# Gated mix of two attentions: three row tiles projected in the main loop instead of ahead of it, and the lead's maxima taken in pairs

## The chip, the cores and the metric

One core of one Trainium2 chip runs the program. The metric is the device time of one execution in microseconds (us): 2651.11 us is the median of three runs of the kernel before (2650.65 to 2652.03). A difference of some 0.2% (5.3 us) is about the least that a measurement of this kernel tells from none.

## The reference

Two attentions over the same 2048 rows x (576 wide), each with 32 heads of 18 elements, are mixed by a gate. A has a key and a value of its own for each head; B shares one key and one value among its 32 heads.

```python
def _A_ref(x, wqkv, wo):          # 32 heads, own k and v each
    scores = jnp.einsum("bhqd,bhkd->bhqk", q, k) * scale
    p = _softmax(scores, axis=-1)
    o = jnp.einsum("bhqk,bhkd->bhqd", p, v)
    return o.transpose(0, 2, 1, 3).reshape(B, S, D) @ wo
def _B_ref(x, wq, wk, wv, wo):    # the same with one k and one v: "bhqd,bkd->bhqk"
...
g = _sigmoid((x * gate_w).sum(-1, keepdims=True))
return g * _A_ref(A_x, ...) + (1 - g) * _B_ref(A_x, ...)
```

## The kernel before

**Number format.** Nearly everything is float32 made of two parts (high and low), so a projection is 14 matrix products: 12 of 128 rows for the first 512 elements of x (high by high, low by high, high by low) and two for the remaining 64, whose high and low parts share one 128-row tile.

**Rows.** All the row vectors that the scores need (B's key, the gate's logit, B's value, B's 32 queries, then query and key of each head of A) stand as 14 tiles of 128 rows in `wall`. Projecting a tile makes 128 x 2048 numbers, in 512-column groups, and sends their high and low parts to `qk_d` in DRAM. From there the main loop loads each head's 18 query rows three times (high, high, low, 54 partitions), and the keys in the same way, on partitions 0 to 53 (`SB`) and again on 64 to 117 (`MB`).

**Stages.** (1) Tiles 0, 1 and 2 are projected while x arrives and is split (`split_x`), 512 columns at a time: order tile 0, 1, 2 within each of four column groups c. PSUM has seven banks to turn through, and the projections use three of them in turn. (2) Tile 3, four groups, during which the rows of tile 0 come back from DRAM (`bring_row`, 26 loads). (3) The **lead**: tiles 4 to 7, sixteen groups; after each group come six matmuls for the row maxima of the first 22 row tiles (`step_max`, L645), which VectorE reduces (L654); ScalarE copies the group out (L300) and GpSimd splits it. `store_x` writes the split x to DRAM for later, eight stores. (4) The **main loop**, 64 heads of 16 steps. Per step: four score matmuls (L690, letter s) on the array's lower 64 rows, beside four for the maxima 22 steps ahead (m) on its upper 64 rows; four exponentials on ScalarE (L698); four reductions on VectorE; and four quarters of the sums with the values (L705, the digits) over all 128 rows. In every second row, one difference product replaces two maxima: x is a product with the difference of two key halves, whose Relu ScalarE writes (L648), and y joins it with the other half in one VectorE instruction (L651): max(a, b) = b + Relu(a - b).

**Units.** What is not attention runs within the main loop as units: 32 of the values of A (14 products), seven for each remaining row tile (14 products of 292 columns), and the output projection (12 products of 288). A unit is executed in 64-row halves (`half_step`, L906): the letters A (rows 64 to 127) and B (rows 0 to 63), each a product of 64 rows, so that they stand beside the scores and maxima. A's sum is copied by ScalarE, B's is added by VectorE (L881).

**Order.** The order on TensorE is written out as strings of eight steps each. PLAIN has no unit, HALF14 one of 14 products, HALF12 one of 12, DENSE four of 12; `emit` chooses by the step T. Per eight steps every string has 32 s, 24 m, 4 x, 4 y and 32 quarters, and the quarters divide it in groups: ten in PLAIN and HALF12, nine in HALF14, seven in DENSE. Six tiles (8 to 13) are units in `row_units`, T from 282 to 618; the values stand from T=18 to 274, the first half of the output projection from 634 to 890, the second in DENSE from 946. A planner (`Clock`) chooses each matmul's PSUM bank as the program is written; it moves nothing on the chip.

Of the kernel before, what the change touches and what calls it, by code (L numbers as in the profile page):

```python
# [8 lines left out]
F32 = mybir.dt.float32  # L9
# [18 lines left out]
LEAD = 22  # L28
PRODS = (("h", "h"), ("h", "l"), ("l", "h"))
# [16 lines left out]
class Clock:  # L46


    def __init__(self):
        self.free = [0.0] * 7  # L50
        self.t = self.act = self.dve = self.last = 0.0
        self.mode, self.begun, self.tail = "", [0.0, 0.0], [0.0, 0.0]
        self.turns, self.count, self.held, self.diffs, self.copies = {"s": 0, "m": 0}, 0, {}, [], []
        self.cleared = 0.0
# [55 lines left out]
    def open(self, part, tile):  # L110
        k, free = self.first()
        self.held[part] = k, self.matmul(tile, free, HALF_MM)
        self.free[k] = 1e15
        return k

    def more(self, part, tile):
        self.held[part] = self.held[part][0], self.matmul(tile, 0.0, HALF_MM)

    def close(self, part):
        k, s = self.held.pop(part)  # L120
        s += HALF_MM - STREAM
        if part == "a":
            end = self.on_act(s, COPY_T) + COPY_T + 55
            self.copies.append(end + 55)
        else:
            self.dve = max(self.dve, self.copies.pop(0))
            end = self.on_dve(s, ADD_T) + ADD_T + 85
# [25 lines left out]
def gated_mix_kernel(ctx: ExitStack, tc: tile.TileContext, xT, wall, wv, wo, out):  # L153
# [15 lines left out]
    kd_d = dram.tile([MT * P, 3, 512], F32, name="kd")  # L169
    m_d = [dram.tile([P, 64], F32, name=f"m_d{i}") for i in range(4)]  # L170
# [55 lines left out]
    stp = ph1.enter_context(tc.tile_pool(name="stp", bufs=3, side="right"))  # L226
    X = {"h": xpool.tile([P, NKT, S], F32R, name="xh"), "l": xpool.tile([P, NKT - 1, S], F32R, name="xl")}
# [18 lines left out]
    def load_w(mt, rest=None):  # L246
        st = wpool.tile([P, NKT, P], F32, name="wst", bufs=6)
# [8 lines left out]
    HAS_K = {0} | {k_row(u) // P for u in range(H, NU)} | {(k_row(u) + DH - 1) // P for u in range(H, NU)}  # L256
# [17 lines left out]
    def leave(mt, c, fp):  # L274
# [3 lines left out]
        if mt == 0 or c == 0 and mt in HAS_K:  # L278
            st = stp.tile([P, 512], F32, name="pst", bufs=3)
            nc.scalar.activation(st, fp, AF.Copy)  # L280
            if c == 0:
                KD[mt] = st
        nc.vector.tensor_tensor(hl[:, 1, :], fp, hl[:, 0, :].bitcast(F32), op=OP.subtract)
        dma(qk_d[:, mt * P:(mt + 1) * P, cs].rearrange("a p f -> p a f"), hl, nc.gpsimd)
        if c == 1 and mt in HAS_K:
            d = stp.tile([P, 512], F32, name="pd", bufs=1)
            nc.vector.tensor_tensor(d, fp, KD.pop(mt), op=OP.subtract)
            dhl = stp.tile([P, 2, 512], F32R, name="pdhl", bufs=1)
            split(d, dhl[:, 0, :], dhl[:, 1, :], nc.scalar, nc.vector)
            dma(kd_d[mt * P:(mt + 1) * P, 0:2, :], dhl, nc.gpsimd)  # L290
            dma(kd_d[mt * P:(mt + 1) * P, 2, :], dhl[:, 0, :], nc.gpsimd)
        if mt == 0:
            dma(z_d[cs], st[ROW_G:ROW_G + 1, :])
            return c, st

    def leave_lead(mt, c, fp):

        hl = stp.tile([P, 2, 512], F32R, name="phl", bufs=4)
        st = stp.tile([P, 512], F32, name="pst", bufs=3)
        nc.scalar.activation(st, fp, AF.Copy)  # L300
        yield
        nc.scalar.activation(hl[:, 0, :], st, AF.Copy)
        nc.gpsimd.tensor_tensor(hl[:, 1, :], st, hl[:, 0, :].bitcast(F32), op=OP.subtract)
        dma(qk_d[:, mt * P:(mt + 1) * P, c * 512:(c + 1) * 512].rearrange("a p f -> p a f"), hl, nc.gpsimd)
        if c == 0:
            KD[mt] = st
        if c == 1:
            d = stp.tile([P, 512], F32, name="pd", bufs=1)
            nc.gpsimd.tensor_tensor(d, st, KD.pop(mt), op=OP.subtract)
            dhl = stp.tile([P, 2, 512], F32R, name="pdhl", bufs=1)  # L310
            split(d, dhl[:, 0, :], dhl[:, 1, :], nc.gpsimd, nc.gpsimd)
            dma(kd_d[mt * P:(mt + 1) * P, 0:2, :], dhl, nc.gpsimd)
            dma(kd_d[mt * P:(mt + 1) * P, 2, :], dhl[:, 0, :], nc.gpsimd)
# [13 lines left out]


    rows_back = []

    def later(o, i):
        rows_back.append(lambda: dma(o, i))

    def bring_row():
        if rows_back:
            rows_back.pop(0)()

    with tc.tile_pool(name="xs", bufs=1, side="right") as xsp:
        XS = []

        def load_x(c, rest=None):
            half = c < 2
            XS.append(xsp.tile([P, NKT, 256 if half else 512], F32, name="xsh" if half else "xs", bufs=2))
# [41 lines left out]
        for mt in range(3, 6):  # L385
# [20 lines left out]
        for c in range(4):  # L406
            for mt in range(3):
                if mt == 2:
                    if c < 3:
                        split_x(2 * c + 2)  # L410
                        split_x(2 * c + 3)
                    shared_v(*keep)
                if c == 0:
                    products(FP[mt], WP[mt], 0, 256, 256)
                    done = leave(mt, c, FP[mt])
                else:
                    done = project(mt, c, WP[mt], 2 if c == 1 and mt == 0 else 1)
                if mt == 0:
                    keep = done
                    if c == 3:  # L420
                        WN = prep_w(W.pop(0))

# [5 lines left out]
    for b in (SB, MB):  # L428
        later(ksb[b + 54:b + 56, :], ones_r)
    load_k(ksb, ROW_KB, put=later)  # L430
    load_kd(kdb, ROW_KB, put=later)
    for u in range(3):
        load_q(u, put=later)


    NT = 8

    def tiles_left(WN):
        for mt in range(3, NT):
            w = WN  # L440
            if mt + 1 < NT:
                WN = prep_w(W.pop(0))
            if mt + 3 < NT:
# [755 lines left out]
```

## Time and profile before

| what | us |
|---|---|
| median of three runs | 2651.11 |
| the profiled execution, its own time | 2651.27 |
| span of that execution, first to last instruction | 2649.5 |
| first exponential of the first eight-step block | 135.49 |
| the 116 blocks from T=18 to T=946 | 2247.54 |
| the seven DENSE blocks after them | 161.42 |

Engines: PE is TensorE (PEld its weight loads), ACT ScalarE, DVE VectorE, POOL GpSimd, SP the engine that only issues DMAs. Rows of the timeline give the start in us, the duration in us, the engine, the line, the operation, what it writes and reads, and how many there are. A table of windows gives for each stretch its length and each engine's busy time, with the number of instructions in brackets, then the granted clock of TensorE, the share of the DMA engines and the rate in GB/s.

### The profile page before, as it was taken

To read this page: it belongs to the slowest core of one execution; us is meant where nothing else is said; L and a number is where in the kernel's file an instruction comes from. 1 tells how busy PE (TensorE), PEld (TensorE's weight loads), DVE (VectorE), ACT (ScalarE), POOL (GpSimd) and SP (SyncE) were. 2 spreads that over 40 slices of the span, in tenths; PEclk is the share of its full clock that TensorE was granted. 3 is DMA by queue.
4 is the path that set the end of the run, shared out by engine and by line. 5 is a ranking of instruction groups with operands and counts; after the bars stand their busy time and mean duration, and the time that the engine had idled before them with its cause. 6 is when DMAs were issued, how large, how long until landed. Compare 5 with 4: busy or idle time off the path is not lost.

```text
span 2649.5 us, 65359 instructions
## 1 busy us (share of the span) xinstructions
PE 2638.3 (100%) x24934; PEld 1396.9 (53%) x24934; DVE 2414.2 (91%) x4557; ACT 2424.7 (92%) x4817; POOL 448.4 (17%) x663
## 2 busy tenths in 40 slices
PE   9999999999999999999999999999999999999998
PEld 7755455554545545455454555545445454445665
DVE  4899999999999999999999999999999999999883
ACT  4399999999999999999999999999999999999887
POOL 2820000110003212322232113000200020112112
PEclk9999999999999999999999999999999999999999
DMA  8831112311124434544564454223322332224312
GB/s 276 331 96 59 51 45 63 81 64 59 55 60 145 134 117 125 162 144 129 154 186 154 150 152 155 83 80 92 100 76 66 90 100 73 82 70 126 109 54 92
DMA packets 190143, 293.94 MB, mean 111 GB/s; under 512 B 54738, under 2 KB 149282, under 8 KB 178252
## 3 DMA queue, kind: packets, MB, share of 16 engines
q1 hardware_dynamic: 170564, 224.02, 28.7%
q0 software_dynamic: 18368, 64.50, 6.5%
q8 instruction: 196, 3.21, 0.5%
q10 hardware_dynamic: 896, 1.23, 0.1%
q14 instruction: 119, 0.97, 0.1%
HBM read 203.29 MB, written 77.62 MB: 106 GB/s over the span
## 4 chain that ended last, share of the span: by engine, by line
PE 99%; DMA 0%; DVE 0%; issue 0%; ACT 0%; POOLq 0%; POOL 0%; ACTq 0%
PE acc L705 39%; PE bank L645 30%; PE bank L690 17%; PE bank L906 8%; PE bank L271 4%; PE bank L886 1%; PE acc L717 1%; DMA xsh<-xT 0%; DVE mx L654 0%; DMA wst<-wall 0%; PE bank L955 0%; PE bank L318 0%; ACT xh L360 0%; POOLq L1195 0%; PE bank L941 0%
## 5 line engine op out<-in xcount | busy, mean ns | idle before, releaser
L698 ACT ACTIVATE pt<-bank 128x512 f32<-128x512 f32 x4096 | 2140.6, 618 | 116.4 <-PE bank L690 71.8
L654 DVE TENSOR_REDUCE mx<-bank 128x1 f32<-128x512 f32 x3096 | 1944.6, 683 | 117.5 <-PE bank L690 56.7
L690 PE MATMUL bank<-qs,ksb 56*128 56x512 f32 x2688 | 902.4, 424 | 0.0
L645 PE MATMUL bank<-ksb,qs 54*128 54x512 f32 x2364 | 818.8, 428 | 0.2
L645 PEld LDWEIGHTS bank<-ksb,qs 54*128 54x128 f32 x2364 | 389.0, 184 | 337.3 <-ACT pt L698 205.6
L705 PE MATMUL acc<-pt,vb 128*19 128x512 f32 (+3 forms) x6216 | 554.5, 452 | 0.0
L705 PE MATMUL acc<-pt,vg 128*19 128x256 f32 (+3 forms) x6096 | 541.0, 449 | 0.0
L690 PEld LDWEIGHTS bank<-qs,ksb 56*128 56x128 f32 x2688 | 439.9, 184 | 155.0 <-DVE mx L654 62.0
L690 PE MATMUL bank<-qs,ksa 56*128 56x512 f32 x1408 | 465.6, 427 | 0.0
L645 PE MATMUL bank<-ksa,qs 54*128 54x512 f32 x1232 | 435.9, 428 | 0.0
L651 DVE CUSTOM_DVE_ANT_0 junk<-bank,xb 128x512 bf16<-128x512 f32 x500 | 342.5, 685 | 21.5 <-PE bank L690 17.0
L648 ACT ACTIVATE xb<-bank 128x512 f32<-128x512 f32 x500 | 293.6, 606 | 7.9 <-PE bank L690 0.2
L645 PEld LDWEIGHTS bank<-ksa,qs 54*128 54x128 f32 x1232 | 204.6, 184 | 161.6 <-ACT pt L698 93.3
L690 PEld LDWEIGHTS bank<-qs,ksa 56*128 56x128 f32 x1408 | 225.0, 184 | 92.4 <-DVE mx L654 31.8
L705 PEld LDWEIGHTS acc<-pt,vb 128*19 128x19 f32 x6216 | 124.4, 97 | 197.5 <-issue 161.6
L705 PEld LDWEIGHTS acc<-pt,vg 128*19 128x19 f32 x6096 | 120.8, 97 | 200.4 <-issue 173.6
L233 POOL CAST mh<-mt 128x32 fp32r<-128x32 f32 x64 | 13.4, 210 | 1190.0 <-DVE mt L663 1190.0
L645 PE MATMUL bank<-kdb,qs 54*128 54x512 f32 x372 | 157.9, 424 | 0.0
L906 PE MATMUL bank<-xr,wrh 64*128 64x292 f32 (+1 forms) x756 | 112.2, 300 | 0.0
L233 POOL CAST rhl<-rst 128x292 fp32r<-128x292 f32 (+2 forms) x54 | 22.5, 417 | 511.5 <-DVE rst L881 467.2
L906 PEld LDWEIGHTS bank<-xr,wrh 64*128 64x128 f32 x756 | 93.0, 186 | 1.8
L645 PEld LDWEIGHTS bank<-kdb,qs 54*128 54x128 f32 x372 | 68.4, 184 | 40.2 <-DVE mx L654 38.4
(144 smaller groups left out, 1924.4 us busy)
## 6 DMA issues: line engine op xcount, KB each, us to landing
qs<-qk SPq DMA_DIRECT2D x384, 144.0 KB
xr<-x_d SPq DMA_DIRECT2D x36, 1314.0 KB
ksa<-qk SPq DMA_DIRECT2D x132, 144.0 KB
qk<-phl POOLq DMA_DIRECT2D x32, 512.0 KB, 6.0
qk<-rhl POOLq DMA_DIRECT2D x36, 292.0 KB, 4.4
ksb<-qk SPq DMA_DIRECT2D x66, 144.0 KB
xv<-x_d SPq DMA_DIRECT2D x16, 576.0 KB
onh<-oh POOLq DMA_DIRECT2D x32, 256.0 KB, 3.8
```

Source lines behind the costliest of these rows:

```text
L233: eng_h.tensor_copy(h, src)
L271: nc.tensor.matmul(fp[:, p0:p0 + g], w[a][:kr, k, :], X[b][:kr, k, x0 + p0:x0 + p0 + g], start=(n == 0), stop=(n == len(PROJ) - 1))
L645: nc.tensor.matmul(pm, qs[u % 3][b:b + 54, i * P:(i + 1) * P], k, start=True, stop=True)
L648: nc.scalar.activation(MX["x", u, i], pm, AF.Relu)
L651: nc.vector.tensor_tensor_reduce(junk, pm, MX.pop(("x", u, i)), 1.0, -3e38, op0=OP.add, op1=OP.max, accum_out=MX[u][:, i, c:c + 1])
L654: nc.vector.tensor_reduce(MX[u][:, i, c:c + 1], pm, axis=AX.X, op=OP.max)
L690: nc.tensor.matmul(ps, kst(u)[b:b + 56, i * P:(i + 1) * P], qs[u % 3][b:b + 56, c * 512:(c + 1) * 512], start=True, stop=True)
L698: nc.scalar.activation(pt, ps, AF.Exp, scale=SCALE)
L705: nc.tensor.matmul(acc[32 * j:32 * j + 19, a:b], v_of(u, i), PT[u, i, j][:, a:b], start=(i == 0), stop=(i == 15), skip_group_check=True)
L717: nc.tensor.matmul(acc[32 * j:32 * j + 19, 256 * half + a:256 * half + b], v_of(NU - 1, i), pt[:, x + a:x + b], start=(i == 0), stop=(i == ...
L886: nc.tensor.matmul(fp[:, 0:u.n], x, y, start=(n == 0), stop=(n == len(u.ops) - 1))
L906: nc.tensor.matmul(u.fp[op][:, 0:u.n], x[b:b + 64], y[b:b + 64], start=(n == 0), stop=(n == last))
```

## The change

`NT` falls from 8 to 5. Tiles 5, 6 and 7 become 21 more units of `row_units`, tiles 3 and 4 become eight units of 512 columns in the lead, and stage (2) is gone.

- **Stage (1).** The order of the twelve groups is now the first one of tiles 0 to 2, then `FIRST`, and x has three buffers of 512 columns instead of two (the weights one less). Tile 0's key and query rows of three heads go to a tensor `kq_d` in the threefold form, so that `rows_back` fetches each set with one DMA (nine where 26 were). The difference of the key's column groups 2 and 3 is made as well (`ke_d`, `keb`).
- **Lead.** Eight units in halves A and B of 512 columns, and between them pairs x and y: all maxima of the first rows are made by difference products, two column groups at a time. The eight stores stand between them (the digit 0).
- **Main loop.** `TWO14` (two units of 14 products, eight groups) in the first six of the value blocks, so that the values end after 26 blocks instead of 32; 63 blocks HALF14 for row tiles, T from 234 to 738; `TWO12` (two units of 12, eight groups) in 16 blocks for the first half of the output projection, T from 754 to 882. From 18 to 946 that makes 83 HALF14 (74 before), 6 TWO14, 16 TWO12 (32 HALF12 before) and 11 PLAIN (10).

```diff
+NT = 5
+FIRST = ((0, 1), (1, 1), (0, 2), (0, 3), (2, 1), (1, 2), (2, 2), (1, 3), (2, 3))
...
-        st = wpool.tile([P, NKT, P], F32, name="wst", bufs=6)
+        st = wpool.tile([P, NKT, P], F32, name="wst", bufs=5)
...
+        dma(kq_d[qr, 1:3, cs], hl[qr])
+        dma(kq_d[qr, 0, cs], hl[qr, 0])
+        dma(kq_d[kr, 0:2, cs], hl[kr])
+        dma(kq_d[kr, 2, cs], hl[kr, 0])
...
-        for c in range(4):
-            for mt in range(3):
-                if mt == 2:
-                    if c < 3:
-                        split_x(2 * c + 2)
-                        split_x(2 * c + 3)
-                    shared_v(*keep)
...
+        for n, (mt, c) in enumerate(FIRST):
+            if n == 1:
+                chunk(2)
+            if n == 2:
+                chunk(3)
+            if mt and keep:
+                shared_v(*keep.pop(0))
+            done = project(mt, c, WP[mt], 2 if n == 0 else 1)
+            if done:
+                keep.append(done)
+            if (mt, c) == (0, 3):
+                rows_back()
...
-NT = 8
...
-    RB = VB + 8 * 33
+    TWICE = [VB + 8 * n for n in range(6)]
+    RB = VB + 8 * (32 - len(TWICE) + 1)
...
+    def lead_max(what, low):
+        M, h = pairs[what].pop(0)
+        u, i = divmod(M, 16)
+        b = SB if low else MB
+        pm = bank_tile(clk.bank(what, 0 if low else 1))
+        k = (kdb, keb)[h][b:b + 54, :] if what == "x" else ksb[b:b + 54, 1024 * h:1024 * h + 512]
+        nc.tensor.matmul(pm, qs[u][b:b + 54, i * P:(i + 1) * P], k, start=True, stop=True)
+        if what == "x":
...
+            nc.scalar.activation(MX["x", M, h], pm, AF.Relu)
+            return
...
+        nc.vector.tensor_tensor_reduce(junk, pm, MX.pop(("x", M, h)), 1.0, -3e38, op0=OP.add, op1=OP.max,
+                                       accum_out=MX[u][:, i, 2 * h:2 * h + 1])
+        if (M, h) == (15, 1):
+            max_rows(0)
...
-    for v in range(16):
-        mt, c, w = next(left)
-        fp = in_turn("s")
-        products(fp, w, c * 512, 0, 512)
-        left_over = leave_lead(mt, c, fp)
...
-        if v < 14:
-            for n, (M, c) in enumerate(banks[6 * v:6 * v + 6]):
-                step_max(*divmod(M, 16), c, c % 2 == 1, "s" if n < 2 else "m")
...
+    lead_steps("AAAAABABABxBABABxBAyxBABAyxBABxy0"
...
+               "sxsyxsyxsyxyy")
...
-        elif VB <= T < VB + 8 * 32 or RB <= T < RE:
+        elif T in TWICE:
+            emit(TWO14, 2)
+        elif VB <= T < RB - 8 or RB <= T < RE:
             emit(HALF14, 1)
-        elif SEG[0][3] + 4 <= T < SEG[0][3] + 4 + 8 * 32:
-            emit(HALF12, 1)
+        elif SEG[0][3] + 4 <= T < SEG[0][3] + 4 + 8 * 16:
+            emit(TWO12, 2)
```

TensorE's queue shows two of the places. First, in stage (1), behind the second column group of tile 0 (`bank0`, two halves of 256 columns; `bank1` and `bank2` are the groups that follow); before:

```order
L271 MATMUL bank0_308<-xl_111,wh_168 128x256 x4
L271 MATMUL bank0_308<-xh_110,wh_168 128x256
L271 MATMUL bank0_308<-xh_110,wl_169 128x256
L271 MATMUL bank1_351<-xh_110,wh_175 128x512 x4
L271 MATMUL bank1_351<-xh_110,wl_176 128x512 x4
L271 MATMUL bank1_351<-xl_111,wh_175 128x512 x4
L271 MATMUL bank1_351<-xh_110,wh_175 128x512
L271 MATMUL bank1_351<-xh_110,wl_176 128x512
L318 MATMUL bank5_376<-ident_83,pst_339 128x18 x4
L271 MATMUL bank2_382<-xh_110,wh_179 128x512 x4
```

The same place in the changed kernel, whose line 311 is the former 318 (transposes of B's value, which read ScalarE's copy `pst` of the group in `bank0`):

```order
L276 MATMUL bank0_311<-xl_114,wh_167 128x256 x4
L276 MATMUL bank0_311<-xh_113,wh_167 128x256
L276 MATMUL bank0_311<-xh_113,wl_168 128x256
L311 MATMUL bank5_364<-ident_85,pst_342 128x18 x4
L276 MATMUL bank1_370<-xh_113,wh_174 128x512 x4
L276 MATMUL bank1_370<-xh_113,wl_175 128x512 x4
L276 MATMUL bank1_370<-xl_114,wh_174 128x512 x4
L276 MATMUL bank1_370<-xh_113,wh_174 128x512
L276 MATMUL bank1_370<-xh_113,wl_175 128x512
L276 MATMUL bank2_395<-xh_113,wh_167 128x512 x4
```

The transposes moved from behind the group of tile 1 to ahead of it, right behind the group whose copy they read; and the group after that (`bank2`) is tile 0 again, with the next column group of x, where it was tile 2 with the same one.

Second, the lead. Before, TensorE's queue held a whole group of 14 products and then six maxima:

```order
L271 MATMUL bank_728<-xh,wh 128x512 x4
L271 MATMUL bank_728<-xh,wl 128x512 x4
L271 MATMUL bank_728<-xl,wh 128x512 x4
L271 MATMUL bank_728<-xh,wh 128x512
L271 MATMUL bank_728<-xh,wl 128x512
L645 MATMUL bank_756<-ksb,qs_89 128x512
L645 MATMUL bank_759<-ksb,qs_89 128x512
L645 MATMUL bank_762<-ksb,qs_89 128x512
```

In the changed kernel a stretch of the lead reads so (L895 is a half product of a unit, L1040 an x when it reads `kdb` or `keb`, a y when it reads `ksb`):

```order
L895 MATMUL bank_672<-xh,wl 128x512
L895 MATMUL bank_693<-xh,wh 128x512
L1040 MATMUL bank_697<-kdb,qs_91 128x512
L1040 MATMUL bank_701<-ksb,qs_91 128x512
L895 MATMUL bank_672<-xh,wl 128x512
L895 MATMUL bank_693<-xh,wh 128x512
L895 MATMUL bank_672<-xh,wl 128x512
L895 MATMUL bank_693<-xh,wh 128x512
L1040 MATMUL bank_709<-ksb,qs_91 128x512
L895 MATMUL bank_693<-xh,wl 128x512
L1040 MATMUL bank_714<-keb,qs_91 128x512
L1040 MATMUL bank_718<-ksb,qs_91 128x512
```

Two units' banks (672 and 693) are open at once, one filled from the lower and one from the upper rows, and the maxima stand singly between the halves instead of six in a row.

212 lines of the change are left out of this document (111 added, 101 removed).

## The prediction

> **What bounds the kernel now.** First the page: busy times and the chain that ended last.
>
> ```profile
> PE 2638.3 (100%) x24934; PEld 1396.9 (53%) x24934; DVE 2414.2 (91%) x4557; ACT 2424.7 (92%) x4817; POOL 448.4 (17%) x663
> PE 99%; DMA 0%; DVE 0%; issue 0%; ACT 0%; POOLq 0%; POOL 0%; ACTq 0%
> ```
>
> TensorE is the path from end to end, with ScalarE and VectorE close behind. So an edit is worth what it does to TensorE's queue, stage by stage. Second, the windows of the start (length, then busy time of PE, PEld, DVE, ACT, POOL):
>
> ```profile
> 6.50:49.75 43.25, 42.32 (x242) 35.95 (x241) 25.86 (x40) 20.08 (x30) 9.12 (x13) 1.00 0.87 290
> 49.75:62.45 12.70, 12.70 (x58) 10.51 (x57) 3.53 (x5) 3.02 (x5) 2.90 (x4) 1.00 0.69 247
> 62.45:126.35 63.90, 63.79 (x296) 45.32 (x294) 55.39 (x91) 19.90 (x34) 49.96 (x63) 1.00 0.89 337
> 126.35:135.49 9.14, 9.14 (x47) 6.04 (x46) 6.75 (x12) 6.84 (x13) 8.06 (x10) 1.00 0.71 264
> ```
>
> Tiles 0 to 2 end at 49.75, tile 3 takes 12.70 (3.18 a group), the lead 63.90, the passage to the main loop 9.14: 85.74 us from 49.75 to the loop's first exponential at 135.49. In the lead TensorE is busy throughout and ScalarE for 19.90 of 63.90.
>
> Third, the blocks of the main loop. These windows count only the exponentials (L698), 32 per eight-step block (the count has one more, which straddles the edge):
>
> ```profile
> 173.42:795.37 621.95, 534.20 (x1025) 1.00 0.20 59
> 795.37:813.91 18.54, 16.67 (x33) 1.00 0.52 156
> 813.91:1631.19 817.28, 700.38 (x1345) 1.00 0.48 147
> 1631.19:1668.29 37.10, 33.33 (x65) 1.00 0.34 114
> 1668.29:2290.94 622.65, 536.86 (x1025) 1.00 0.28 83
> 2290.94:2420.96 130.02, 116.69 (x226) 1.00 0.34 97
> 2420.96:2582.38 161.42, 121.10 (x225) 1.00 0.27 86
> ```
>
> They are, in order: 32 HALF14 at 19.44 us each, a PLAIN at 18.54, 42 HALF14 at 19.46, two PLAIN at 18.55, 32 HALF12 at 19.46, seven PLAIN at 18.57, seven DENSE at 23.06. One unit costs a block 0.88 us; each of the three further units of DENSE costs (23.06 - 19.46) / 3 = 1.20.
>
> **Term 1, stage (1): +2.65 us.** The same twelve groups and four sets of transposes; only the waits differ. Rows around the place shown above, of the kernel before:
>
> ```profile
> 22.21 1.88 SPq L159 DMA_DIRECT2D xs<-xT  x3
> 22.56 1.09 PE L271 MATMUL bank<-xh,wh 128*128 128x512 f32 x4
> 23.25 0.59 ACT L280 ACTIVATE pst<-bank 128x512 f32<-128x512 f32 x1
> 25.20 0.63 ACT L231 ACTIVATE pdhl<-pd 128x512 fp32r<-128x512 f32 x1 [1.36 <-DVE pd L287]
> 25.85 0.42 PE L318 MATMUL bank<-ident,pst 18*128 18x18 f32 x4
> 26.50 2.43 ACT L360 ACTIVATE xh<-xs 128x1280 fp32r<-128x1280 f32 x2
> 27.80 1.23 DVE L366 TENSOR_TENSOR xl<-xs,xh 128x1024 fp32r<-128x1024 f32 x1 [0.47 <-ACT xh L360]
> 29.05 0.42 DVE L370 TENSOR_TENSOR xh<-xs,xh 64x256 fp32r<-64x256 f32 x1
> ```
>
> (a) The transposes now follow at 22.5 the group whose copy `pst` ends at 23.84: a wait to about 24.0, 1.4 us; the whole of TensorE's queue stands behind it. The tile 1 group then runs 24.4 to 27.6. (b) Tile 0's third column group follows, and needs `xh`: ScalarE's split (2.43) can start when `pdhl` is done at 25.83, ends at 28.3: 0.7 us. (c) The fourth needs `xl` 1.8 us after its start. VectorE needs 1.23 + 0.42 twice for each column group, 3.3 us, two of them behind each other with one subtraction between: done at 34.2, wanted at 33.4: 0.8 us. Then everything is resident and the old 3.18 pace returns: 22.56 + eight groups 25.5 + three sets of transposes of 0.45 + 1.4 + 0.7 + 0.8 = 52.4 instead of 49.75. The last x load (`xs`, issued at 22.21, after a buffer came free) has a buffer of its own now and starts earlier, so DMA ends no wait here. Bounds: nothing (the waits overlap) to +5.
>
> **Term 2, the lead: 45.6 us where 85.7 stood.** Halves of 512 columns don't occur in the trace, so the nearest rows are score and maximum beside each other, 512 columns, 56 and 54 rows:
>
> ```profile
> 1225.55 0.39 PE L690 MATMUL bank<-qs,ksb 56*128 56x512 f32 x1
> 1225.55 0.39 PE L645 MATMUL bank<-ksb,qs 54*128 54x512 f32 x1
> 1225.78 0.39 PE L690 MATMUL bank<-qs,ksb 56*128 56x512 f32 x1
> 1225.78 0.45 PE L645 MATMUL bank<-ksb,qs 54*128 54x512 f32 x1
> ```
>
> Both row halves start one each 0.23 us. Counted in the string up to the last unit, the upper rows get 104 A, 42 x and 4 Y (a y on the upper rows), the lower ones 112 B and 37 y: 150 and 149 slots, 150 x 0.233 = 35.0 us, and 0.2 for the lower rows' late start. Beside it: VectorE has 41 joins, eight adds, a weight split and the first maxima.
>
> ```profile
> 1222.40 0.68 DVE L651 CUSTOM_DVE_ANT_0 junk<-bank,xb 128x512 bf16<-128x512 f32 x1
> 1223.01 6.07 DVE L654 TENSOR_REDUCE mx<-bank 128x1 f32<-128x512 f32 x10
> 132.80 2.08 ACT L698 ACTIVATE pt<-bank 128x512 f32<-128x512 f32 x4
> ```
>
> A join gives way after 0.61: 41 x 0.61 + 8 x 0.69 + 1.3 = 32 us of 35. ScalarE: 50 copies and Relus at 0.5 and a split, 26. TensorE bounds it, but VectorE has a tenth of slack, so I add 1.5 for local waits: 36.7, end of the units at 89.1. GpSimd was busy 49.96 us for some 15 groups in the old lead, 3.3 each, against 4.6 us per unit now.
>
> ```profile
> x_d<-xh POOLq DMA_DIRECT2D x4, 1280.0 KB, 8.0
> x_d<-xl POOLq DMA_DIRECT2D x4, 1024.0 KB, 5.9
> qk<-phl POOLq DMA_DIRECT2D x17, 512.0 KB, 5.6
> ```
>
> These eight stores and eight groups (4 x 1280 + 4 x 1024 + 8 x 512 KB) are 13.6 MB in 37 us, about the 337 GB/s of the old lead; they land about when the lead ends, and the first units that read the stored x are two blocks further.
>
> The first scores then need the maxima of the first head. This chain stands in the old lead:
>
> ```profile
> 113.38 0.21 DVE L661 TENSOR_REDUCE m<-mx 128x16 f32<-128x64 f32 x1
> 116.52 0.22 POOL L233 CAST mh<-mt 128x32 fp32r<-128x32 f32 x1
> 117.10 0.33 SPq L159 DMA_DIRECT2D m_d<-mh  x1
> 120.94 1.26 SPq L159 DMA_DIRECT2D qs<-m_d  x2
> ```
>
> From the reduction to the last row load's issue it took 8.8 us, 2.7 of it in GpSimd's queue; landing is estimated at 2.8, a little under the 3.5 that the step before took after its issue. In the new string 37 slots (8.6 us) stand between the 32nd join, which completes the head, and the first s; the chain needs 1.0 (join) + 0.5 + 0.8 + 3.8 + 1.3 + 2.8 = 10.2 with a free GpSimd. I take 1.2 us of waiting (0 to 4 by the rows: all of GpSimd's 2.7 again is the upper end), queued behind the score: all of TensorE. Then eight exponentials and six Relus at 0.52 (row above) and 0.4 of latency until the block's own first exponential, 7.7. Sum: 36.7 + 1.2 + 7.7 = 45.6, so that exponential stands at 52.4 + 45.6 = 98.0 instead of 135.49. Terms 1 and 2 together: **-37.5 us**. Bounds -41 to -29: no waits at all, or 5 us more in the lead and 3 in stage (1).
>
> **Term 3, the main loop: +21 us.** Two units in one block with eight groups are in no row; they lie between HALF and DENSE. How a block is made up shows in one group with a unit and one without:
>
> ```profile
> 1224.44 0.84 PE L705 MATMUL acc<-pt,vb 128*19 128x384 f32 x8
> 1225.21 0.50 PE L690 MATMUL bank<-qs,ksb 56*128 56x512 f32 x1
> 1230.54 0.50 PE L645 MATMUL bank<-ksb,qs 54*128 54x512 f32 x1
> 1234.48 0.84 PE L705 MATMUL acc<-pt,vb 128*19 128x384 f32 x8
> 1226.16 0.85 PE L705 MATMUL acc<-pt,vb 128*19 128x128 f32 x16
> ```
>
> Three pairs without a unit take 1225.21 to 1226.16 = 0.95 (three slots of 0.23 and 0.25 for the change of mode); the group with 14 products 3.94, that is on the upper rows eight slots of 0.23, 13 of 0.14 and the 0.25. Three quarters take 0.77, 0.13 over their stream: a group costs about 0.37 beside its work. With halves of 0.135 (288 columns are a little shorter than 292): TWO12 against HALF12, 12 slots more and two groups fewer, 19.46 + 1.62 - 0.74 = 20.34; against DENSE, 24 slots fewer and one group more, 23.06 - 3.24 + 0.37 = 20.19. I take 20.3. TWO14 against HALF14, 14 slots more and one group fewer, 20.97; against DENSE, 20 slots fewer and one group more, 20.73. I take 20.85. Ends: 20.05 and 20.6 for the two if a group is worth more, and 20.65 (HALF plus 1.20) and 21.1 on the straight line from HALF to DENSE.
>
> Before, T=18 to 946: the first six of the seven windows, 2247.54 us. After: 83 x 19.45 + 11 x 18.57 + 6 x 20.85 + 16 x 20.3 = 1614.4 + 204.3 + 125.1 + 324.8 = 2268.6. Difference **+21.1 us** (+15.6 to +28.2). The 21 added units pay for themselves at 1.0 us, against 3.18 times four sevenths = 1.8 us of the same columns in the lead. DENSE and the end are untouched.
>
> **Sum.** 2651.27 (own time of the profiled execution, 1.8 over its span) - 37.5 + 21.1 = 2634.9; the median is 0.16 lower. I say 2635.
>
> **A rule against it.** The rows of the joins and exponentials above say that TensorE stays the bound in the lead by a tenth. The Trainium skill, TensorEngine Tiling (Array Packing), section PSUM Bottleneck, warns that tiling speeds up the matmuls but not the evacuation of PSUM, which may become the bound; here each unit leaves two banks instead of one. By the rows of this trace that is a rival of its own, first below.
>
> **Rivals.**
> *Evacuation sets the lead.* If a join holds VectorE for its full 0.68 and the read of its accumulator, and waits for its Relu, 41 x 0.77 + 5.5 + 1.3 = 38, and waits for the seven banks, two of them held by the open units, come on top: 42 for the lead instead of 36.7, 2640. For it: VectorE at nine tenths. Against: rows at 0.61.
> *The rows come late.* Tile 0 now ends at 35.6, its last writes are issued by about 41 and land 3.5 later, and reads of up to 442 KB (54 x 2048 x 4) follow; at 0.25 of the 0.29 MB/us that this stage moved in all, the first four (1.3 MB with the short ones) land at about 50, 2 us ahead of need. Late by 4: 2639.
> *Two units crowd a block.* On the straight line of 1.20 per unit: 16 x 0.35 + 6 x 0.25 = +7, 2642. Against: DENSE itself has four.
> *Slower: two 512-column halves do not run beside each other.* Then 299 slots follow each other, 70 us for 35: 2670. It decides from the slot where the lead costs 16.2 us more, (35 + 16.2) / 150 = 0.34 us. For it: no row has two full-length 64-row products. Against: the group of 3.94 us holds 27 halves and 15 maxima or scores, whose streams in a row would be 6.5.
> *Better.* No wait in stage (1) and for the maxima, short blocks: 2626.
>
> **Chances.** Forecast (2630 to 2638) 0.45; evacuation 0.16; late rows 0.10; crowded blocks 0.12; better 0.08; no overlap, or a stall of such a size elsewhere, 0.09. Range 2626 to 2645: the better case and the three small rivals, two of them together. Faster by over 0.2% (about what a measurement tells from none; below 2645.8) 0.85, within 0.07, slower 0.08.
>
> **What the profile after would show.** The first exponential of the loop at 98; the second column group's transposes waiting for ScalarE's `pst` for 1.4 us; the upper and lower halves of L895 at 0.23; VectorE below TensorE in the lead; the first score waiting about 1 us for `qs<-m_d`; the eight-step blocks at 20.3 and 20.85. Wrong if the lead is over 45 us, if the units' halves start 0.3 apart, or if the two-unit blocks exceed 21.

## The result: 0.8% slower, and where the time stands in the profile after

The changed kernel takes **2672.16 us** (median of four runs, 2670.40 to 2673.68), the kernel before 2650.99 us beside it: a ratio of 1.0079 (95% interval 1.0062 to 1.0096). The forecast was 2635.0 us, 2626 to 2645: wrong in sign as well as in size. The profiled execution took 2673.68 us, 2.0 over its span.

Table of the forecast's own markers, in us:

| marker | forecast | measured | too low by |
|---|---|---|---|
| stage (1) ends, lead begins | 52.4 | 53.65 | 1.25 |
| lead: from there to the first score | 36.7 + 1.2 | 47.05 (to 100.70) | 9.15 |
| from there to the loop's first exponential | 7.7 | 13.99 (to 114.69) | 6.3 |
| blocks T=2 and T=10, taken as unchanged | 19.40 + 18.52 | 33.61 + 18.99 | 14.7 |
| T=18 to T=946 | 2268.6 | 2275.15 | 6.5 |
| DENSE, end, and what lies around the span | 230.3 | 231.2 | 0.9 |

The sum is 38.8 us, the whole distance between 2634.9 and 2673.7. The page alone does not tell it: TensorE is still the path.

```profile
PE 2638.8 (99%) x25413; PEld 1421.9 (53%) x25413; DVE 2395.4 (90%) x4581; ACT 2448.6 (92%) x4855; POOL 482.6 (18%) x725
PE 96%; DMA 1%; POOL 0%; DVE 0%; issue 0%; SPq 0%; ACT 0%; POOLq 0%; ACTq 0%; DVEq 0%
```

In the chain, TensorE's 99% have become 96%: some three per cent of the path now belongs to other things. The start of the span is where they are. Windows of the changed kernel (length, busy time of PE, PEld, DVE, ACT, POOL, granted clock, DMA share, GB/s):

```profile
6.50:53.65 47.15, 44.18 (x244) 36.25 (x242) 27.25 (x42) 21.25 (x32) 7.62 (x11) 1.00 0.85 257
53.65:60.00 6.35, 2.58 (x17) 1.79 (x17) 0.69 (x1) 1.09 (x2) 0.44 (x1) 0.90 0.66 255
60.00:70.00 10.00, 9.98 (x58) 8.04 (x58) 6.40 (x17) 6.48 (x12) 4.30 (x13) 0.72 0.77 293
70.00:100.40 30.40, 30.00 (x227) 22.47 (x225) 25.89 (x73) 21.06 (x37) 20.74 (x26) 1.00 0.90 343
100.40:114.69 14.29, 9.69 (x50) 4.88 (x47) 9.48 (x23) 8.38 (x20) 4.19 (x6) 0.95 0.57 209
114.69:148.30 33.61, 23.28 (x174) 10.87 (x174) 15.98 (x32) 18.38 (x37) 10.71 (x11) 0.71 0.27 77
148.30:167.29 18.99, 18.92 (x192) 9.49 (x192) 18.13 (x34) 18.59 (x39) 0.47 (x2) 1.00 0.17 50
```

Three rows are ill: at the lead's start TensorE works 2.58 us of 6.35, in the passage 9.69 of 14.29, and in the loop's first block 23.28 of 33.61, each with a low granted clock in it or behind it. The timeline names what each waited for (start, duration, engine, line, and in brackets the idle time before it and what ended it):

```profile
60.02 0.76 PE L1040 MATMUL bank<-keb,qs 54*128 54x512 f32 x1 [3.79 <-DMA keb<-ke]
...
114.46 0.22 ACT L452 ACTIVATE g<-z 128x16 f32<-128x16 f32 x1 [4.93 <-DMA z<-z_d]
...
131.78 0.35 DVE L456 RECIPROCAL g<-g 128x32 f32<-128x32 f32 x1 [11.20 <-POOL g L454]
...
132.74 0.79 PE L679 MATMUL bank<-qs,ksb 56*128 56x512 f32 x1 [9.70 <-DVE mx L643]
```

The last three belong together. `g` and `z` are the gate: L452 is its exponential on ScalarE, L454 an addition on GpSimd, L456 the reciprocal on VectorE. In the kernel before these three stood at 89.00, 96.34 and 96.70 us, in the lead. Now ScalarE waits 4.93 us for `z` ahead of the loop's first exponential, and VectorE waits 11.20 us for GpSimd, with a block's maxima queued behind the reciprocal and TensorE behind their banks. The two queues in which it hangs, SyncE's and GpSimd's:

```profile
111.28 1.12 SPq L162 DMA_DIRECT2D ksa<-ones_r  x4
112.44 0.35 SPq L162 DMA_DIRECT2D z<-z_d  x1
```

```profile
119.26 0.91 POOL L239 CAST vwh<-vg 128x864 fp32r<-128x864 f32 x1 [13.17 <-PE bank L634]
...
129.49 1.40 POOL L241 TENSOR_TENSOR vwl<-vg,vwh 128x576 fp32r<-128x576 f32 x1
130.83 0.64 POOL L591 MEMSET vst<- 128x304 f32 x2
131.45 0.30 POOL L454 TENSOR_SCALAR g<-g 128x32 f32<-128x32 f32 x1
```

The load of `z` is issued behind `ksa`, whose memory is free only when the last store of x has landed: SyncE waited 12.3 us for it, and the chain that ended last holds this store up to the issue of `ksa`:

```profile
105.32 5.40 DMA x_d<-xl
```

The gate's addition, 0.30 us long, stands behind 11.6 us of splitting the value weights (1.5 us of these are a wait for their load). The cause is five lines of the removed lead loop, which the diff ahead of the prediction does not show:

```diff
-        if v >= 4 and slow:
-            try:
-                next(slow[0])
-            except StopIteration:
-                slow.pop(0)
```

`slow[0]` is at this point the generator `gates()`, whose five steps are these instructions. The new lead never steps it, so `begin` does, at T=0, 2, 4 and on.

In the main loop (exponentials of L687 only: six TWO14, 63 HALF14, sixteen TWO12, eight PLAIN, seven DENSE):

```profile
167.29:292.02 124.73, 104.05 (x193) 1.00 0.23 71
...
699.03:1925.78 1226.75, 1050.83 (x2017) 1.00 0.50 150
1963.34:2293.95 330.61, 270.17 (x513) 1.00 0.30 88
2293.95:2442.44 148.49, 133.15 (x257) 1.00 0.32 93
2442.44:2603.86 161.42, 121.05 (x225) 1.00 0.28 86
```

That is 20.79, 19.47, 20.66, 18.56 and 23.06 us per block.

### The profile page after: what moved, and what is told of

The parts are those of the page before. It is cut to its first block, busy times and chain, and to the rows that moved or that the text cites. A ratio compares the mean times of both kernels' runs of the same rounds, so it can differ in the third digit from the quotient of the medians.

```text
span 2671.7 us, 66517 instructions
## 1 busy us (share of the span) xinstructions
PE 2638.8 (99%) x25413; PEld 1421.9 (53%) x25413; DVE 2395.4 (90%) x4581; ACT 2448.6 (92%) x4855; POOL 482.6 (18%) x725
## 4 chain that ended last, share of the span: by engine, by line
PE 96%; DMA 1%; POOL 0%; DVE 0%; issue 0%; SPq 0%; ACT 0%; POOLq 0%; ACTq 0%; DVEq 0%
PE acc L694 38%; PE bank L634 28%; PE bank L679 18%; PE bank L895 10%; PE acc L706 1%; DMA keb<-ke 1%; PE bank L1040 1%; PE bank L875 0%; DMA x_d<-xl 0%; POOL vwl L241 0%; DMA kq<-phl 0%; DMA vg<-wv 0%; DVE mx L643 0%; SPq L162 0%; POOL vwh L239 0%
## 5 line engine op out<-in xcount | busy, mean ns | idle before, releaser
L687 ACT ACTIVATE pt<-bank 128x512 f32<-128x512 f32 x4096 | 2145.3, 613 | 131.6 <-PE bank L679 79.4
L643 DVE TENSOR_REDUCE mx<-bank 128x1 f32<-128x512 f32 x3002 | 1885.8, 683 | 129.7 <-PE bank L634 58.8
L694 PE MATMUL acc<-pt,vb 128*19 128x256 f32 (+3 forms) x6168 | 555.3, 455 | 0.1
L694 PE MATMUL acc<-pt,vg 128*19 128x512 f32 (+3 forms) x6120 | 531.8, 447 | 0.0
L634 PE MATMUL bank<-ksa,qs 54*128 54x512 f32 x1232 | 442.1, 427 | 0.0
L239 POOL CAST rhl<-rst 128x292 fp32r<-128x292 f32 (+2 forms) x81 | 34.0, 420 | 780.4 <-DVE rst L870 704.7
L895 PE MATMUL bank<-xr,wrh 64*128 64x292 f32 (+1 forms) x1134 | 167.7, 300 | 0.0
L895 PEld LDWEIGHTS bank<-xr,wrh 64*128 64x128 f32 x1134 | 139.3, 186 | 2.8
L895 PE MATMUL bank<-xr,wrl 64*128 64x292 f32 (+1 forms) x567 | 102.3, 294 | 0.0
```

The lines of the kernel that those rows point to most:

```text
L239: eng_h.tensor_copy(h, src)
L634: nc.tensor.matmul(pm, qs[u % 3][b:b + 54, i * P:(i + 1) * P], k, start=True, stop=True)
L643: nc.vector.tensor_reduce(MX[u][:, i, c:c + 1], pm, axis=AX.X, op=OP.max)
L687: nc.scalar.activation(pt, ps, AF.Exp, scale=SCALE)
L694: nc.tensor.matmul(acc[32 * j:32 * j + 19, a:b], v_of(u, i), PT[u, i, j][:, a:b], start=(i == 0), stop=(i == 15), skip_group_check=True)
L895: nc.tensor.matmul(u.fp[op][:, 0:u.n], x[b:b + 64], y[b:b + 64], start=(n == 0), stop=(n == last))
```

## The experiments

Unless said otherwise, each is the changed kernel with the edit shown, timed in five rounds against the kernel before (medians of 2651.45 to 2652.10 us in these).

**Gates in the lead.** The theory: the gates' waits in the loop's first blocks make the change slower, because the queues of SyncE and GpSimd hold other work ahead of them there. The rival: that other work (stores of x, value weights) is late in the new order anyway, and whoever comes next would wait.

```diff
             elif op in "0123":
                 store_x(stores.pop(0))
+                if len(stores) < 6 and slow:
+                    try:
+                        next(slow[0])
+                    except StopIteration:
+                        slow.pop(0)
```

> The changed kernel, with the five steps of the gates (load of z, two Exp on ScalarE, the add on GpSimd, the reciprocal on VectorE, the stores) taken one by one in the lead again, at the third to seventh store of x, as the removed lead took them. Theory (the gates were left to the first blocks of the loop, where their waits stand in the engines' queues): the wait of ScalarE for z (4.9 us before the loop) and that of the reciprocal for GpSimd (11.2 us in the first block) go; the loop's first block of 33.62 us comes back to about 19.4 us; time 2672.2 - 14 to 20 = 2652 to 2658 us. Rival (the first block is long because GpSimd's stores of x and its splitting of the value weights come later than before, whoever waits for them): 2669 to 2673 us, and the block stays above 30 us.

Measured: **2654.43 us**, 1.0007 (0.9998 to 1.0016) of before, 17.8 us under the changed kernel. The windows of the blocks T=2 and T=10 (exponentials only) show where:

```profile
106.91:127.48 20.57, 16.66 (x33) 0.89 0.40 118
127.48:146.49 19.01, 16.82 (x33) 1.00 0.17 50
```

Block T=2 takes 20.57 us instead of 33.61, and the loop begins at 106.91 instead of 114.69; 2.7 us of that lie in the lead, where the wait for `keb` was 2.12 us this time. The splitting of the value weights is still there, and nobody waits behind it. The rival falls.

**The same part alone, in the kernel before.** The removed lines above are taken out of the kernel before, and nothing else.

> The kernel before, with one thing removed: its lead no longer steps the gates, so that they begin with the loop, as in the changed kernel. Theory: the loop's start and first block take 14 to 20 us more, the block at T=2 goes from 19.40 to about 33 us, time 2665 to 2671 us. Rival (the gates cost this only behind the new, shorter lead): 2651 to 2654 us.

Measured: **2671.85 us**, 1.0074 (1.0061 to 1.0087): 20.4 us slower, a little more than the 14 to 20 expected, by an edit that moves a handful of tiny instructions. Its timeline has the same two waits:

```profile
142.74 0.21 ACT L463 ACTIVATE g<-z 128x16 f32<-128x16 f32 x1 [7.34 <-DMA z<-z_d]
```

```profile
159.58 0.35 DVE L467 RECIPROCAL g<-g 128x32 f32<-128x32 f32 x1 [10.72 <-POOL g L465]
```

So the loss is no property of the new lead. The loop starts 7.5 us later (142.96 instead of 135.49), block T=2 takes 32.19 instead of 19.40.

**Rows earlier.** `keb`, fifth of the row loads, goes second.

```diff
         load_kd(kdb, ROW_KB)
+        dma(keb[MB:MB + 54, :], ke_d.rearrange("p a f -> (p a) f"))
         q(0, MB)
```

> The changed kernel, with the load of keb moved from the fifth to the second place among the loads of rows. Theory (the lead's matmuls wait for rows that come at 0.15 MB/us, keb as the last that the first pairs need): the wait of 3.79 us at 60 us goes, most of the low granted clock behind it too (0.92 and 0.72 until 70 us), the lead's end comes 3 to 7 us earlier: 2665 to 2669 us. Rival (the next row load, that of ksb, takes keb's place as the last one, or VectorE sets the lead's end anyway): within 1.5 us of 2672.2, with a wait of 2 to 4 us for other rows.

Measured: **2670.14 us**, 1.0068 (1.0054 to 1.0082). In the trace the wait for `keb` is gone, the granted clock from 60 to 70 us is 1.00, and the lead is done at 97.3 instead of 100.7; then a wait of 2.10 us for the maxima stands ahead of the first score at 99.43. The 2.0 us lie between the two expectations (3 to 7 us less, or within 1.5), and the intervals of the two ratios overlap: the time alone would not settle it. The wait is not steady either: with the same order of loads it was 3.79 us in the changed kernel, 2.1 with the gates in the lead, and 0.6 in the next experiment. And the rival had a point: with `keb` second the next load, `ksb`, is the last to come, with a wait of 0.7 us here and of 0.2 to 4.4 us in the kernels below.

**Two buffers for the joins.** In the changed kernel's lead consecutive joins (L1049, each with the read of its accumulator) stand 0.87 us apart:

```profile
98.36 0.68 DVE L1049 CUSTOM_DVE_ANT_0 junk<-bank,xd 128x512 bf16<-128x512 f32 x1
98.96 0.08 DVE L1049 DVE_READ_ACCUMULATOR2_ANT mx<- 128x1 f32 x1
99.22 0.69 DVE L1049 CUSTOM_DVE_ANT_0 junk<-bank,xd 128x512 bf16<-128x512 f32 x1 [0.17 <-ACT xd L1044]
99.83 0.08 DVE L1049 DVE_READ_ACCUMULATOR2_ANT mx<- 128x1 f32 x1
100.09 0.69 DVE L1049 CUSTOM_DVE_ANT_0 junk<-bank,xd 128x512 bf16<-128x512 f32 x1 [0.17 <-DVE mx L1049]
```

```diff
-        junk = lead.tile([P, 512], BF16, name="junk", bufs=1)
+        junk = lead.tile([P, 512], BF16, name="junk", bufs=1) if M > LEAD else \
+            xdp.tile([P, 512], BF16, name="junk2", bufs=2)
```

> The changed kernel, with two buffers in turn for the tile that the lead's joins write and nobody reads. Theory (consecutive joins stand 0.87 us apart because each waits until its forerunner has left the one buffer): pitch 0.61 to 0.70 us, the lead's end 6 to 10 us earlier, 2662 to 2667 us. Rival A (the pitch is the join's own length with the read of its accumulator): pitch 0.87 and 2672 us. Rival B (pitch falls, but matmuls at the low granted clock then set the lead): 2668 to 2672 us.

Measured: **2668.04 us**, 1.0060 (1.0048 to 1.0073). The joins with two buffers (L1050):

```profile
81.53 0.69 DVE L1050 CUSTOM_DVE_ANT_0 junk<-bank,xd 128x512 bf16<-128x512 f32 x1
82.15 0.08 DVE L1050 DVE_READ_ACCUMULATOR2_ANT mx<- 128x1 f32 x1
82.15 0.69 DVE L1050 CUSTOM_DVE_ANT_0 junk<-bank,xd 128x512 bf16<-128x512 f32 x1
82.76 0.08 DVE L1050 DVE_READ_ACCUMULATOR2_ANT mx<- 128x1 f32 x1
82.76 0.69 DVE L1050 CUSTOM_DVE_ANT_0 junk<-bank,xd 128x512 bf16<-128x512 f32 x1
```

The pitch is 0.61: the 0.26 us were the wait for the one buffer, and rival A falls. The time lies at the edge of rival B's range, but the granted clock was 1.00 from 54 to 90 us, so its mechanism falls too. But TensorE's waits say why 4 us came out of it and not 8 (line, releaser; us in total, times, longest):

```profile
PE bank L679 <- DVE mx L643: 8.5, 1, 8.5
PE bank L679 <- DMA qs<-m_d: 7.5, 1, 7.5
```

The first score was due at 92.3 and then waited 7.5 us for the maxima of the first head, until 99.73. Neither rival had this: the shorter lead runs into the next wait. The first row is the gates' wait, still there.

**The three edits together.**

> The changed kernel with three edits together: the gates stepped in the lead (alone 2654.4, -17.8 us), keb loaded second (alone -2.0), two buffers for the joins' unread tile (alone -4.1). Theory 1 (the gains belong to different waits and add up): 2672.2 - 17.8 - 2.0 - 4.1 = 2648.3 us. Theory 2 (a shorter lead only ends in the wait of the first score for the maxima, 7.46 us with two buffers alone, which the stores of x hold in the DMA queues, so that the gain of keb is lost and part of the others): 2650 to 2653 us, with a wait of 8 to 10 us of TensorE for the rows of maxima at about 90 us.

Measured: **2657.71 us**, 1.0022 (1.0013 to 1.0031): above both expectations, and 3.3 us above the kernel with the gates alone (the two intervals just overlap, so the trace has to tell). T=18 begins at 149.72 instead of 146.49. The maxima leave at 88.73, 2 us earlier than with the gates alone (90.81), but the first exponential of the passage starts later (100.99 for 98.97), and the granted clock behind the wait falls to 0.50 (below). That gains in different waits add up was wrong; that a wait for the maxima takes them back is right, and it took back more than them.

**What holds the maxima.** The last three stores of x are moved behind the lead's units (on top of the three edits).

```diff
-               "AyABABxBAyABxBABABYyABxBABAyxBABABABxy0"
+               "AyABABxBAyABxBABABYyABxBABAyxBABABABxy"
...
-               "sxsyxsyxsyxyy")
+               "000sxsyxsyxsyxyy")
```

> The three edits, and the last three of the eight stores of x (1.05 MB each) moved behind the lead's last unit, so that the maxima's store and loads have fewer bytes ahead of them. Theory (the maxima travel for 14 us, 85.65 to 99.7 with two buffers alone, because the stores of x fill the DMA engines): first score 4 to 7 us earlier than in the kernel with the three edits, time 4 to 6 us below it. Rival A (all of x is out as late as before or later, and the loop's first tiles and loads wait for its memory): the first exponentials of the loop no earlier, time within 1 us of that kernel or above it. Rival B (the maxima's own small packets set their time): the wait stays.

Measured: **2655.64 us**, 1.0012 (1.0003 to 1.0020), 2 us under the three edits; first score's wait 2.4 us instead of 4.6. The intervals of the two overlap, and it is less than the theory gave: the maxima's store still took 5.9 us to land, with the DMA engines 0.73 busy and five stores of x issued before it. The rows' wait at the lead's start was 4.4 us in this run and 1.3 in the other, so the two times do not compare the maxima alone. A clearer cut moves all eight behind the lead; the gates get a letter of their own, g, at five of the places where a 0 stood:

```diff
-               "AyABxBABAyABxBAyABxBAyABxBABAyxBABAyxB0"
+               "AyABxBABAyABxBAyABxBAyABxBABAyxBABAyxBg"
...
-               "sxsyxsyxsyxyy")
+               "00000000sxsyxsyxsyxyy")
```

> The three edits, with all eight stores of x (9.4 MB) issued behind the lead's last unit, and the gates stepped at five marks of the lead as before. Theory (the stores of x fill the DMA engines in the lead, so that rows come late at its start and the maxima late at its end): the rows' wait at 55 to 60 us below 2 us, the maxima's store lands within 3 us of its issue instead of 4.9, the first score does not wait for them, the first exponential of the loop at 99 to 104 us (110.04 with the stores at their marks), time 2646 to 2651 us. Rival (the loop's tiles and its first loads then wait for the memory of x, free only at about 120 us): blocks T=2 to T=18 longer by 5 to 15 us, 2656 to 2670 us.

Measured: **2670.10 us**, 1.0070 (1.0057 to 1.0082). SyncE's queue with the three edits, then with all stores behind (the loads `qs<-m_d` are issued when the store `m_d` has landed):

```profile
88.73 0.34 SPq L162 DMA_DIRECT2D m_d<-mh  x1
93.58 2.03 SPq L162 DMA_DIRECT2D qs<-m_d  x2
```

```profile
89.23 0.34 SPq L162 DMA_DIRECT2D m_d<-mh  x1
91.07 1.26 SPq L162 DMA_DIRECT2D qs<-m_d  x2
...
129.22 1.13 SPq L162 DMA_DIRECT2D ksa<-ones_r  x4
```

4.85 us became 1.84, the first score did not wait, and the loop began at 104.69: so far the theory holds. Between issue and landing the DMA engines were 0.98 busy in the first case and 0.26 in the second. Stores of x at their marks do not always cost this, though: in the changed kernel the maxima's store took 1.93 us, with the DMA engines 0.49 busy, although a store of x had been issued 0.07 us ahead of it. The Trainium skill, DMA: Bandwidth & Descriptors, section Queues, rings and completion order, says that each DMA engine takes turns between its queues by whole packets. That a small transfer then shares its engines with a bulk one is inferred from this; the 1.84 and 4.85 us would fit it. But then the last store lands at 129, everything in SyncE's queue behind `ksa` waits for it, and the block T=10 takes 38.12 us:

```profile
PE bank L679 <- DMA qs<-m_d: 17.1, 1, 17.1
```

Here it is the second head's maxima. The rival's mechanism is right too, at another place than it said. One part of the theory fell: the rows' wait at the lead's start stayed at 2.2 us with no store of x in the queues. SyncE's own queue moves the rows slowly: 1.84 MB from 46 to 60 us in the changed kernel, 0.13 MB/us, and its first store of x is issued only at 61 us.

**Three stores at their marks, five behind the lead.**

> The same with the first three stores of x at their marks and five behind the lead. Theory (what counts is how many bytes stand ahead of the maxima at 88 us): the rows' wait at the start as in the kernel with the three edits (1.3 to 4.4 us), the maxima without wait, time between the kernel with all stores behind and the one with the three edits. Rival (the memory of x decides): better than the kernel with all eight behind.

Measured: **2658.19 us**, 1.0025 (1.0015 to 1.0034). The loop begins at 101.16, the earliest so far, and block T=10 takes 28.06 us: 6.6 us of waiting for the second head's maxima, which stand behind the value weights in the queues of SyncE and GpSimd. The first head's maxima came without a wait, as the theory had it, and its time lies between the two others, but with their order turned round: that the kernel with all stores behind would be the fastest was wrong. Being 12 us under that kernel, and next to the three edits, is what the rival said.

**Value weights later.** The same kernel, with the loads and the splitting of the value weights begun at T=10 instead of T=2, behind the second head's maxima:

```diff
-    when(2, lambda: begin_units(value_units()))
+    when(10, lambda: begin_units(value_units()))
```

> The three edits, three stores of x at their marks and five behind the lead, and the value weights' loads and splitting begun at T=10 instead of T=2, behind the second head's maxima in the queues of SyncE and GpSimd. Theory (the block at T=10 took 28.06 us because the second head's maxima stand in these two queues behind loads that wait for the last store of x): that block 19.0 to 19.5 us, T=18 begins at about 141 us, time 4 to 9 us under the kernel with three stores at their marks: 2649 to 2654 us. Rival (the weights come too late for the first units instead): the wait moves to the blocks at T=18 and T=26, 5 us or more there, time 2655 to 2659 us.

Measured: **2648.42 us**, 0.9987 (0.9978 to 0.9996). Block T=10 takes 19.02, T=18 begins at 142.89, and the first units do not wait. This version is the first under the kernel before, by 3.6 us: the interval ends just below 1, but the difference is smaller than the 5.3 us named at the start as the least that a measurement tells from none.

**The clock.** First, with the three edits, 20 pairs of filler matmuls (`keep_busy`) stand ahead of the first score, where TensorE waits:

> The three edits, and 20 more pairs of the filler matmuls (512 and 256 columns on a constant; about 6.6 us at full clock, their result is never used) ahead of the first score, where TensorE waits for the maxima. They take nothing away and are there to see the granted clock. Theory (the low granted clock in the 10 us behind a long wait, 0.50 with two buffers alone and 0.72 with the gates in the lead, comes from TensorE's idleness): 0.9 or more from 100 to 110 us, 1 to 3 us below the kernel with the three edits. Rival (it does not come from the idle time): clock as there, time the same, or above by what the filler outlasts the wait.

Measured: **2657.16 us**, 1.0019 (1.0010 to 1.0028), as with the three edits. Windows of the three edits, then with the filler:

```profile
90.00:100.00 10.00, 5.62 (x48) 4.69 (x44) 6.00 (x18) 4.57 (x8) 8.45 (x11) 0.88 0.95 349
100.00:110.00 10.00, 9.77 (x35) 7.27 (x36) 5.72 (x15) 7.14 (x14) 0.42 (x1) 0.50 0.67 224
```

```profile
90.00:100.00 10.00, 10.00 (x75) 9.08 (x73) 6.15 (x18) 4.57 (x8) 8.42 (x11) 1.00 0.98 364
100.00:110.00 10.00, 9.08 (x49) 6.91 (x47) 5.38 (x15) 6.51 (x14) 0.58 (x1) 0.93 0.68 232
```

The clock is held (0.93 for 0.50) and block T=2 takes 19.34 us for 20.68, but the filler outlasts the wait: the first score's exponential is 1.7 us later, which eats the gain. The Trainium skill, TensorE: Matmul & The Clock Gate, section Why this matters for your kernels, warns of idle gaps above about 3 us; the wait of 3.79 us with 0.72 behind it and this pair of runs agree.

A long gap is not needed, though. With the value weights later, the clock stood at 0.50 from 100 to 106 us, and TensorE had no wait above 0.2 us in the ten us ahead of that. There the filler was put between the scores:

```diff
-               "00000sxsyxsyxsyxyy")
+               "00000sxfsyxfsyxfsyxfyyf")
```

> The kernel with the value weights later, and five more pairs of filler matmuls among the scores and pairs of the passage from the lead to the loop, where 9 to 11 matmuls start in 2 us instead of 20 and the granted clock stands at 0.50 from 100 to 106 us although TensorE waits for nothing longer than 0.2 us. Theory (the clock falls with the density of matmuls, not with waits alone): 0.9 or more from 100 to 106 us, and 1 to 2.5 us less than 2648.4. Rival (it has another cause): the clock stays at 0.50 there, time the same or up to 1.5 us more for the filler.

Measured: **2647.69 us**, 0.9983 (0.9974 to 0.9992), the lowest of all; the 0.7 us from the kernel without this filler is inside their spread. The window without it and with it:

```profile
100.00:106.00 6.00, 5.84 (x26) 3.05 (x23) 4.49 (x9) 4.62 (x9) 3.27 (x5) 0.50 0.99 347
```

```profile
100.00:106.00 6.00, 6.00 (x51) 2.76 (x53) 5.01 (x11) 5.79 (x13) 1.35 (x2) 1.00 1.02 362
```

Full clock, and block T=2 takes 18.53 us instead of 19.97. The two windows do not hold the same work, since with the filler the passage stands 1.9 us earlier (first score at 93.27 instead of 95.16, most of it a shorter wait for the rows); but there the clock was 1.00 in each 2 us from 92 to 112. Over eleven runs of each kernel the granted clock of the whole span was 0.9973 on average without the filler and 0.9983 with it. So the filler goes with a held clock.

What brings the fall stays open. The number of starts alone does not: the changed kernel passed from 100 to 106 us at a clock of 1.00 with 32 matmuls in that window, as many as stood from 94 to 100 us ahead of this fall. Nor does the length of one wait: at the lead's start the clock stayed at 1.00 behind a wait of 2.12 us (gates in the lead) and fell to 0.50 from 59 to 65 us behind one of 1.12 us (value weights later).

## Why the prediction was wrong

**The step that failed.** Term 2 ended with "Then eight exponentials and six Relus ... 7.7", and the sum took the blocks T=2 and T=10 as they were. Both rest on an inventory of what the new lead issues; it held TensorE's slots, the joins, the copies and the stores, but not what the old lead did besides, the stepping of the gates. No rival named it: "a stall of such a size elsewhere" had a few per cent, without a place. It cost 4.93 us in the passage and 14.2 us in block T=2, together 19.1; putting it back gained 17.8 us (20.5 between the profiled executions, 2.7 of them in the lead by a shorter wait for `keb`), and taking it out of the kernel before cost 20.4. Without it the change would have come out even with before, not 0.6% faster, so two more steps were off.

**Term 2, the lead (9.15 us too short).** "The first four land at about 50, 2 us ahead of need" was wrong: SyncE's queue moved 0.13 MB/us where 0.25 was taken, and the rival of late rows, priced at 4 us, came true with a wait of 3.79. With `keb` second the lead was done 3.4 us earlier (97.3 for 100.7). "A join gives way after 0.61" came from a row in which a reduction follows the join. A join behind a join waits for the one buffer that both write, 0.87. The rival that evacuation sets the lead was therefore right in that VectorE's joins set it, and near in size (42 us against 43.6 with `keb` second), but not in its reason: the join's own length with its read was not what held them. In the six kernels with `keb` second, two buffers and no filler ahead of the first score the lead was done 39.0 to 43.2 us after its start, 4 to 8 us below the 47.05; the longer ones are those with the longer waits for rows (0.2 to 4.4 us). So these two terms make up between half and nearly all of the 9.15 us.

**Term 2, the maxima.** 1.2 us of waiting were forecast; there was none, since the lead was too long to expose it. (The terms as written, 10.2 less 8.6, give 1.6.) In the shorter leads it came out at 2.1 to 7.5 us: the estimate's order of events was right, and its "2.8 to land" too short with stores on their way (4.6 us with the three edits, from the end of the loads' issue to the first score).

**Term 3 (6.5 us too short).** TWO14 came out at 20.79 (20.85 forecast). TWO12 took 20.66, where 20.3 was chosen and 20.65 was the straight line's end: 16 x 0.36 = 5.8 us of the 6.5. The rival of crowded blocks was right for these blocks alone. Why the second unit costs 1.2 us there, no run was made to tell.

**What held.** The transposes of stage (1) waited 1.18 us for ScalarE's copy (1.4 forecast), the products behind them 0.47 for `xh` (0.7) and 0.78 for `xl` (0.8):

```profile
24.62 0.42 PE L311 MATMUL bank<-ident,pst 18*128 18x18 f32 x4 [1.18 <-ACT pst L285]
28.93 1.20 PE L276 MATMUL bank<-xh,wh 128*128 128x512 f32 x4 [0.47 <-ACT xh L365]
35.03 1.20 PE L276 MATMUL bank<-xl,wh 128*128 128x512 f32 x4 [0.78 <-DVE xl L371]
```

That the stage still ended 1.25 us late has another reason: the group ahead of these transposes was through some 0.7 us later than in the kernel before. Why, no run was made to tell. And the slower rival, that 512-column halves do not overlap, fell: upper and lower ones start in pairs, and 0.23 us later the next pair.

```profile
97.59 0.39 PE L895 MATMUL bank<-xh,wl 64*128 64x512 f32 x1
97.60 0.39 PE L895 MATMUL bank<-xh,wh 64*128 64x512 f32 x1
97.83 0.40 PE L895 MATMUL bank<-xh,wl 64*128 64x512 f32 x2
```

So the trade at the heart of the change works. With its side effects mended the kernel measured 0.17% under the one before, which is less than a measurement surely tells from none: T=18 begins at 139.4 instead of 173.4 us, and the 21 units in the main loop take back some 28 of these 34 us.

## What to carry to other kernels

When a loop is removed, list everything that it issued on every queue, above all the calls that have nothing to do with its purpose: a 0.3 us instruction that landed behind 11.6 us of other work in GpSimd's queue, with a tiny load behind a bulk store in SyncE's, cost some 20 us here. When a stage is shortened, look up what its length was hiding (stores that hold memory, a small transfer among large ones, a tile with one buffer), since each of these became the next wait. And take a pitch between two instructions from a row where the same two follow each other.

## What the runs showed of the hardware

- The granted clock fell to 0.50 for 6 us with no wait of TensorE above 0.2 us in the ten us ahead of it (value weights later), and stayed at 1.00 with five more pairs of fillers in that passage. It also stayed at 1.00 in the changed kernel's passage, with as many matmuls as there were ahead of the fall, and behind a wait of 2.12 us at the start of one lead, where it fell behind 1.12 us in another. What it goes by stays open.
- A store of the maxima on SyncE's queue landed 1.84 us after its issue with the DMA engines 0.26 busy, 1.93 us at 0.49, and 4.85 us at 0.98, with GpSimd's bulk stores in flight.
- Two consecutive joins that write the same unread buffer stand 0.87 us apart, with two buffers 0.61.
